# Gated linear attention and two mixture layers on one core: 32-wide column tiles in the attention step, and experts' places counted in steps of 8 tokens

## The chip, the cores and the metric

One core of a Trainium2 chip runs the whole program in one launch. The metric is the time of one execution in microseconds of device time. Of the kernel before, three timed runs are shown, and one profiled execution from which every row below is taken.

## The reference

Three layers follow one another over 3072 tokens (4 batches of 768) of 320 numbers (8 heads of 40).

1. A gated recurrence. For each head, a state `C` of 40 x 40 and a sum `n` of 40 are updated at every token, and the output is a ratio:

```
C = f_stab * C + i_stab * outer(v_t, k_t);   n = f_stab * n + i_stab * k_t
y_t = sigmoid(o_t) * (C @ q_t) / max(|n . q_t|, 1)
```

2. A dense layer: `h = x @ w_in` (320 to 1024), `h * softmax(h)`, a layer norm with the scale `g_ln`, `@ w_out` (1024 to 320).

3. A routed layer: each token goes to the one of 8 experts whose embedding has the largest cosine with it, and gets `gate * (relu(x @ w1[e]) @ w2[e])`, with the softmax of the scaled cosines as its gate.

Inputs and outputs are 32-bit floats.

## The kernel before, in words

**First half.** The sequence is cut into 24 chunks of 128 tokens (6 to a batch), and layers 1 and 2 are done chunk by chunk. For a chunk the recurrence becomes four groups of small fp32 matmuls on TensorE: `scores` (k against q, 128 x 128 for each head), `values` (the masked scores against the values, 41 columns with the row sum), `carried` (q against the state of the chunks before, 82 columns for two heads) and `outer` (k against the values, into the state). A matmul's output can stand on a part of the 128 partitions; that part is its column tile, and matmuls on different column tiles of the array can run beside each other. `values` and `carried` put a chunk's 128 tokens out in two halves of 64; `outer` puts the 40 rows of two heads at partitions 0 and 64. In the step `att` of the order, PE runs the rest of the dense layer's first product of an earlier chunk, then the next chunk's scores, then this chunk's values, carried state and outer product. The dense layer splits each operand in a high and a low part of the type fp32r and sums three products.

**Between the halves.** Tokens are routed in groups of 4 or 2 chunks (`r_best` to `r_add`). Each token's place within its expert is counted by matmuls with triangular matrices, and one-hot matmuls turn "token to place" into "place to token" (`inv`, from which `columns` reads gather indices). The experts are ranked by their count: the first two ranks by the count after 4 groups, the others by the final one (`rank_all`).

**Second half.** Each rank has a fixed number of places (`CAPS`, in units of `CW` = 32 tokens). A rank is a unit of work; rank 0 is two units, of which the first (384 tokens, `u0`) needs only the tokens of the first 5 groups, so it can start early. For a unit, rows of `ys` are gathered by an indirect DMA (`x_get`), transposed and split (`x_tr`, `x_hi`, `x_lo`); `m1` gives for each of 8 blocks `f` of the hidden layer 8 matmuls that stream the unit's tokens; `m1_hi` on ACT and `m1_lo` on DVE take the relu out of PSUM in two parts; `m2` gives for each tile of 128 tokens 24 matmuls that stream 320 columns; ACT applies the gate and an indirect DMA scatters the rows. Where a unit leaves a half tile of 64, the high and the low part of that half stand side by side as one 128-wide operand (16 matmuls instead of 24), and DVE adds the two halves of the result (`y_add`).

Tokens beyond the places are done by a loop at the end, that runs as often as a table on the chip says (`over_table`, 35 instructions on DVE, in the steps `otab`); with none left over, it runs no time.

**The order.** Every step is given to a plan with its engine and what it needs; the order in which they are issued is written out as numbers (`AT`, about 20 to a microsecond), and each engine runs its steps in that order. Steps that use the same PSUM bank wait for each other.

Of the kernel before, what the change touches and what calls it, by code (L numbers as in the profile page):

```python
# [9 lines left out]
F32 = mybir.dt.float32  # L10
F32R = mybir.dt.float32r
BF16 = mybir.dt.bfloat16
I32 = mybir.dt.int32
# [26 lines left out]
YW = XW + 1  # L40
# [5 lines left out]
CAPS = (16, 14, 14, 14, 12, 11, 11, 10)  # L46
CW = 32
NT = tuple(-(-x * CW // P) for x in CAPS)
# [3 lines left out]
NOVF = 32  # L52
GMAX = 40.0

C_ID, C_IOT, C_I192, C_I8, C_TOK, C_U, C_J, C_R, C_CAP, C_HCAP, C_TRI, C_GL, C_TAU = 0, 128, 256, 448, 456, 480, 608, 640, 648, 656, 664, 792, 800
NCONST = 801
# [4 lines left out]
EP = 32  # L61
FUSE = 2
# [1587 lines left out]
```

## Time and profile before

| | |
|---|---|
| median of 3 runs | 539.2 us (538.67 to 540.77) |
| profiled execution | 537.65 us |
| its span, first to last instruction | 535.7 us |
| busy share of PE, PEld (weight loads), DVE, ACT, POOL | 96%, 88%, 63%, 51%, 37% |
| TensorE clock granted | 0.994 of 2.4 GHz over the span |

PE is TensorE's matmul, PEld its weight loads, DVE VectorE, ACT ScalarE, POOL GpSimd, SP SyncE. A row of the timeline merges like instructions that follow one another: start, length from the first start to the last end, engine, line, output<-inputs, rows*columns of the weights and the shape streamed, and their count. Matmuls are pipelined: one lasts longer than the distance at which the next can start. L671 is line 671 of the kernel.

### The profile page before, as it was taken

What the parts mean: (1) busy time and instruction counts of PE and PEld (TensorE: products, weight loads), DVE (VectorE), ACT (ScalarE), POOL (GpSimd) and SP (SyncE); (2) the same over time, 40 slices, a digit from 0 to 9 for tenths busy, and PEclk for the clock granted to TensorE, in tenths of its full rate; (3) what the DMA queues carried; (4) which work ended last, traced back from release to release, by engine and by line L of the source; (5) the groups of instructions that cost most, each with busy time, mean ns of one, the idle gap of its engine ahead of it and who ended that gap; (6) DMA issues with size and microseconds to landing.
All of it is one profiled execution on the core that took longest, in us unless ns stands there. A gap on an engine that the chain in (4) does not pass through costs nothing. (4 is left out here: it accounts for less than half of the span.)

```text
span 535.7 us, 11869 instructions
## 1 busy us (share of the span) xinstructions
PE 512.6 (96%) x4600; PEld 470.5 (88%) x4600; DVE 339.5 (63%) x750; ACT 275.0 (51%) x601; POOL 198.0 (37%) x355
## 2 busy tenths in 40 slices
PE   5999999999999999999999889999999999999991
PEld 3778888999889999889998679899999999999991
DVE  6997756775667766667766867878463437554420
ACT  3464654655546574565547665454454345544420
POOL 2026222462174247226315864734243223202102
PEclk9999999999999999999999999999999999999997
DMA  8914423153242333314400631658364345723000
GB/s 335 406 44 139 130 78 117 50 167 111 81 133 80 118 116 128 125 38 136 169 1 1 217 114 61 201 176 253 106 187 157 104 124 176 249 54 129 13 20 31
DMA packets 20401, 67.95 MB, mean 127 GB/s; under 512 B 2635, under 2 KB 5779, under 8 KB 20336
## 3 DMA queue, kind: packets, MB, share of 16 engines
q1 hardware_dynamic: 17360, 58.14, 33.3%
q0 software_dynamic: 2976, 8.96, 5.1%
q8 instruction: 38, 0.62, 0.5%
q14 instruction: 27, 0.22, 0.1%
HBM read 58.43 MB, written 8.91 MB: 126 GB/s over the span
## 5 line engine op out<-in xcount | busy, mean ns | idle before, releaser
L1203 DVE SCALAR_TENSOR_TENSOR uu<-hpu,uu 128x384 fp32r<-128x384 f32 (+3 forms) x104 | 40.0, 415 | 55.2 <-ACT uu L1198 48.8
L1235 POOL DMA_INDIRECT out_x<-you,sidx x28 | 28.4, 1013 | 109.6 <-ACT you L1228 101.4
L1198 ACT ACTIVATE uu<-hpu 128x448 fp32r<-128x448 f32 (+4 forms) x72 | 33.9, 473 | 60.6 <-PE hpu L1186 53.0
L782 PE MATMUL Y<-OH,uh 128*128 128x328 f32 x192 | 63.4, 330 | 0.0
L1221 PE MATMUL ypu<-hr,uu 128*128 128x320 f32 (+1 forms) x192 | 59.8, 311 | 0.8 <-DVE uu L1203 0.8
L783 PE MATMUL Y<-OL,uh 128*128 128x328 f32 x192 | 60.0, 313 | 0.0
L784 PE MATMUL Y<-OH,ul 128*128 128x328 f32 x192 | 59.9, 312 | 0.0
L1223 PE MATMUL ypu<-hr,uu 128*128 128x320 f32 (+1 forms) x192 | 59.3, 309 | 0.0
L1222 PE MATMUL ypu<-lr,uu 128*128 128x320 f32 (+1 forms) x192 | 59.2, 309 | 0.0
L1140 DVE TENSOR_TENSOR lr<-wr,hr 128x1024 fp32r<-128x1024 f32 (+1 forms) x32 | 43.2, 1356 | 19.3 <-ACT hr L1133 18.4
L1182 PE MATMUL hpu<-exhr,hr 128*128 128x448 f32 (+4 forms) x144 | 49.6, 344 | 0.3 <-DVE uu L1203 0.3
L1184 PE MATMUL hpu<-exlr,hr 128*128 128x448 f32 (+4 forms) x144 | 48.0, 333 | 0.2 <-issue 0.2
L1183 PE MATMUL hpu<-exhr,lr 128*128 128x448 f32 (+4 forms) x144 | 48.0, 333 | 0.0
L1133 ACT CAST hr<-wr 128x1024 fp32r<-128x1024 f32 (+1 forms) x40 | 44.6, 1136 | 5.7 <-DMA wr<-in_w 1.6
L774 DVE TENSOR_TENSOR ul<-tpu,uh 128x512 fp32r<-128x512 f32 x48 | 32.5, 688 | 22.1 <-ACT uh L770 21.8
L733 DVE TENSOR_REDUCE nmx<-H 128x1 f32<-128x1024 f32 x24 | 29.3, 1222 | 25.7 <-PE H L729 23.7
L738 ACT ACTIVATE e<-H,nmx 128x1024 f32<-128x1024 f32 x24 | 26.8, 1116 | 36.6 <-DVE nmx L733 36.6
L720 PE MATMUL H<-WH,xh 128*128 128x512 f32 x96 | 39.9, 416 | 0.0
L1149 POOL DMA_INDIRECT xgr<-ys,gidx x28 | 31.6, 1129 | 18.5 <-DVE sidx L1070 6.6
L721 PE MATMUL H<-WL,xh 128*128 128x512 f32 x96 | 37.6, 391 | 0.0
L770 ACT CAST uh<-tpu 128x512 fp32r<-128x512 f32 x48 | 27.6, 587 | 18.4 <-PE tpu L766 17.3
L782 PEld LDWEIGHTS Y<-OH,uh 128*128 128x128 f32 x192 | 36.1, 188 | 0.8
(258 smaller groups left out, 1356.7 us busy)
## 6 DMA issues: line engine op xcount, KB each, us to landing
qk<-in_qkT SPq DMA_DIRECT2D x24, 512.0 KB
wr<-in_w SPq DMA_DIRECT2D x24, 512.0 KB
nat<-in_nat SPq DMA_DIRECT2D x24, 484.0 KB
wr<-in_w SPq DMA_DIRECT2D x16, 640.0 KB
ys<-yr SPq DMA_DIRECT2D x5, 770.0 KB
rawwo<-in_w_out SPq DMA_DIRECT2D x4, 640.0 KB
rawwi<-in_w_in SPq DMA_DIRECT2D x5, 512.0 KB
ys<-yr SPq DMA_DIRECT2D x2, 385.0 KB
```

The lines of the kernel that those rows point to most:

```text
L782: T.matmul(out=yp, lhsT=uh, rhs=OH[:, k, :], start=(k == 0), stop=False)
L783: T.matmul(out=yp, lhsT=uh, rhs=OL[:, k, :], start=False, stop=False)
L784: T.matmul(out=yp, lhsT=ul, rhs=OH[:, k, :], start=False, stop=(k == 7))
L1133: A.copy(out=R.h[i], in_=R.raw[i])
L1140: eng.tensor_tensor(out=R.l[i], in0=R.raw[i], in1=R.h[i].bitcast(F32), op=ALU.subtract)
L1182: T.matmul(out=o, lhsT=R.h[k][:, fs_], rhs=xh[:, k, tk], start=(k == 0), stop=False)
L1183: T.matmul(out=o, lhsT=R.l[k][:, fs_], rhs=xh[:, k, tk], start=False, stop=False)
L1184: T.matmul(out=o, lhsT=R.h[k][:, fs_], rhs=xl[:, k, tk], start=False, stop=False)
L1203: V.scalar_tensor_tensor(out=l_part(U, f, a, b), in0=U.us["p", f][:, a:b], scalar=0.0, in1=U.us["u", f][:, a:b].bitcast(F32), op0=ALU.max, ...
L1221: T.matmul(out=yp, lhsT=uh, rhs=hi, start=(f == 0), stop=False)
L1222: T.matmul(out=yp, lhsT=uh, rhs=lo, start=False, stop=False)
L1223: T.matmul(out=yp, lhsT=ul, rhs=hi, start=False, stop=(f == 7))
```

## The change

Four things, and with them a new set of numbers in `AT` (nearly every step of the second half and many of the first stand at other places).

1. `values`, `carried` and `outer` use column tiles of 32 instead of 64: four calls where there were two.
2. `CAPS` is in tokens, in multiples of 8. The remainder of a unit may be any width up to 64; its low part is put at column 64 of the operand. The unit `u1` (112 places) streams the high and the low part of x in one matmul, and adds the two results with one more step on ACT (`m1_part`) and one on DVE (`m1_sum`). In the last unit the split tile comes first.
3. `over_table` and its steps are gone; six small instructions say whether any expert has more tokens than places. If so, a loop runs every expert over every chunk with a mask (also used when the gates need the other path). For it, each row of `ys` has one more column, the expert's number.
4. Constants and tiles that only the table used are gone.

```diff
-CAPS = (16, 14, 14, 14, 12, 11, 11, 10)
-CW = 32
+CAPS = (496, 432, 448, 424, 360, 352, 328, 264)
+CT = [slice(EP * c, EP * c + EP) for c in range(4)]
...
     def values(s, num, stop):
         for p in range(NP):
             for r in range(2):
-                for j in range(2):
-                    T.matmul(out=num[halves(j), 2 * p + r, :], lhsT=s["Pt"][:, r, p, halves(j)], rhs=s["vp"][:, 2 * p + r, :], ...)
+                for q in CT:
+                    T.matmul(out=num[q, 2 * p + r, :], lhsT=s["Pt"][:, r, p, q], rhs=s["vp"][:, 2 * p + r, :], ...)
 
     def carried(s, num, c, start):
         for p in range(NP):
-            for j in range(2):
-                T.matmul(out=num[halves(j), 2 * p:2 * p + 2, :], lhsT=s["qk"][:QR, 0, p, halves(j)], rhs=c[:, p, :], ...)
+            for q in CT:
+                T.matmul(out=num[q, 2 * p:2 * p + 2, :], lhsT=s["qk"][:QR, 0, p, q], rhs=c[:, p, :], ...)
 
     def outer(s, stc, start, stop):
         for p in range(NP):
-            for r in range(2):
-                T.matmul(out=stc[HP * r:HP * r + D, p, :], lhsT=s["k"][:, 2 * p + r, :], rhs=s["vp"][:, 2 * p + r, :], ...)
+            for r, (a, b) in ((r, x) for r in range(2) for x in ((0, 32), (32, D))):
+                T.matmul(out=stc[HP * r + a:HP * r + b, p, :], lhsT=s["k"][:, 2 * p + r, a:b], rhs=s["vp"][:, 2 * p + r, :], ...)
...
-            self.half, self.lo = w % P == HP, EARLY * P if name == "u0" else 4 * P
+            self.left, self.lo, self.small = (w % P if w % P <= HP else 0), (EARLY if name == "u0" else 4) * P, w <= P
...
+        if U.small:
+            both = hp[:, :2 * U.w].rearrange("p (a t) -> p a t", a=2)
+            for k in range(2):
+                T.matmul(out=both, lhsT=R.h[k][:, fs_], rhs=R.x["b"][:, :, k, tk], start=(k == 0), stop=False)
+                T.matmul(out=o, lhsT=R.l[k][:, fs_], rhs=xh[:, k, tk], start=False, stop=False)
+            T.matmul(out=both, lhsT=R.h[2][:, fs_], rhs=R.x["b"][:, :, 2, tk], start=False, stop=True)
+            return
...
+    def m1_part(U, f):
+        U.us["s", f] = small.tile([P, P], F32, tag="hs", name=f"hs{U.name}_{f}", bufs=4)
+        A.copy(out=U.us["s", f][:, :U.w], in_=U.us["p", f][:, U.w:2 * U.w])
+
+    def m1_sum(U, f):
+        s_ = U.us["s", f][:, :U.w]
+        V.tensor_tensor(out=s_, in0=s_, in1=U.us["p", f][:, :U.w], op=ALU.add)
...
-            if both:
-                u = U.us["u", f][:, t0:t0 + P]
+            if both:
+                u = U.us["u", f][:, t0:t0 + HP + n]
                 T.matmul(out=yp, lhsT=u, rhs=hi, start=(f == 0), stop=False)
                 T.matmul(out=yp, lhsT=u, rhs=lo, start=False, stop=(f == 7))
...
+        jo = U.tiles if u < len(units) - 1 else (U.tiles[-1],) + U.tiles[:-1]
...
+    def too_many():
+        q, w = od["q"], ordw
+        V.tensor_tensor(out=q, in0=perm[:, 1].rearrange("p r c -> p c r"), in1=crow.unsqueeze(1).broadcast_to([P, E, E]), op=ALU.mult)
+        V.tensor_reduce(out=w[:, 0, :], in_=q, axis=AX.X, op=ALU.add)
+        V.tensor_tensor(out=w[:, 1, :], in0=w[:, 3, :], in1=w[:, 0, :], op=ALU.is_gt)
+        V.tensor_tensor(out=w[:, 1, :], in0=w[:, 1, :], in1=few, op=ALU.max)
+        V.tensor_reduce(out=w[:, 2, 0:1], in_=w[:, 1, :], axis=AX.X, op=ALU.max)
+        V.tensor_scalar(out=again, in0=w[0:1, 2, 0:1], scalar1=widef, scalar2=None, op0=ALU.max)
...
-            nv = nc.values_load(nov[0:1, 0:1], min_val=0, max_val=NOVF - 1)
-            with tc.For_i(0, nv, 1) as j:
...
+            with tc.For_i(0, E, 1) as e:
...
+                with tc.For_i(0, NG, 1) as g:
...
+                    V.scalar_tensor_tensor(out=part_of, in0=R.x[0][:, XE:YW], scalar=mine, in1=R.x[0][:, XW:XE], op0=ALU.is_equal, op1=ALU.mult)
...
+                    V.scalar_tensor_tensor(out=o, in0=U.us["y", 0][:, :DM], scalar=part_of, in1=o, op0=ALU.mult, op1=ALU.add)
```

## Rows read from the trace of the kernel before

**Rows 1.** The page's part 1: busy us (share of the span) xinstructions.

```profile
PE 512.6 (96%) x4600; PEld 470.5 (88%) x4600; DVE 339.5 (63%) x750; ACT 275.0 (51%) x601; POOL 198.0 (37%) x355
```

**Rows 2.** Windows: length, busy us (xcount) by engine, clock, DMA share, GB/s.

```profile
10.00:45.00 35.00, 34.93 (x376) 27.26 (x375) 32.77 (x55) 19.42 (x53) 9.86 (x9) 1.00 0.59 227
...
200.00:250.00 50.00, 50.00 (x531) 45.55 (x532) 33.50 (x81) 28.59 (x72) 22.51 (x48) 1.00 0.34 111
...
290.00:320.00 30.00, 25.96 (x163) 22.77 (x162) 23.39 (x54) 20.66 (x43) 21.20 (x35) 1.00 0.45 147
...
450.00:500.00 50.00, 50.00 (x333) 49.67 (x332) 28.29 (x38) 26.67 (x43) 7.30 (x8) 1.00 0.44 137
```

**Rows 3.** PE's waits: who waited <- releaser: us, times, longest.

```profile
PE ip L875 <- POOL ohv L869: 1.6, 1, 1.6
PE txr L1160 <- DMA xgr<-ys,gidx: 1.5, 1, 1.5
```

**Rows 4.** Timeline of PE in one chunk's attention step: start us, us, what.

```profile
207.77 1.13 PE L671 MATMUL num<-nat,Pt 128*64 128x41 f32 x32
208.72 0.77 PE L676 MATMUL num<-Cb,qk 104*64 104x82 f32 x16
209.32 0.48 PE L681 MATMUL stc<-nat 128*40 128x41 f32 x16
209.73 0.42 PE L782 MATMUL Y<-OH,uh 128*128 128x328 f32 x1
```

**Rows 5.** Groups by form: rows*columns of weights, streamed, xcount | busy us, mean ns.

```profile
L671 PE MATMUL num<-nat,Pt 128*64 128x41 f32 x768 | 27.2, 231 | 0.0
L676 PE MATMUL num<-Cb,qk 104*64 104x82 f32 x320 | 15.4, 238 | 0.0
L681 PE MATMUL stc<-nat 128*40 128x41 f32 x320 | 9.6, 202 | 0.0
...
L553 PE MATMUL wep<-wt,enT 128*32 128x128 f32 x32 | 1.3, 279 | 0.0
...
L671 PEld LDWEIGHTS num<-nat,Pt 128*64 128x64 f32 x768 | 24.3, 138 | 3.8 <-ACT OH L600 0.8 <-issue 0.4
...
L553 PEld LDWEIGHTS wep<-wt,enT 128*32 128x32 f32 x32 | 0.8, 109 | 0.2
```

**Rows 6.** wep, on four column tiles: timeline, then a window of 0.03 us.

```profile
16.14 1.00 PE L553 MATMUL wep<-wt,enT 128*32 128x128 f32 x24
...
16.14:16.17 0.03, 0.03 (x4) 0.03 (x4) 0.00 (x0) 1.00 0.78 307
```

**Rows 7.** Timeline of m1: a block's matmul and the next block's, 8 matmuls on.

```profile
347.40 0.28 PE L1183 MATMUL hpu<-exhr,lr 128*128 128x128 f32 x1
...
348.29 0.28 PE L1183 MATMUL hpu<-exhr,lr 128*128 128x128 f32 x1
...
425.31 0.36 PE L1182 MATMUL hpu<-exhr,hr 128*128 128x448 f32 x1
...
426.93 0.37 PE L1182 MATMUL hpu<-exhr,hr 128*128 128x448 f32 x1
...
500.55 0.31 PE L1182 MATMUL hpu<-exhr,hr 128*128 128x320 f32 x1
...
501.72 0.31 PE L1182 MATMUL hpu<-exhr,hr 128*128 128x320 f32 x1
```

**Rows 8.** Groups by form of the small unit's passes out of PSUM.

```profile
L1198 ACT ACTIVATE uu<-hpu 128x128 fp32r<-128x128 f32 x8 | 2.1, 278 | 6.2 <-PE hpu L1186 2.7 <-issue 1.8 <-PE txr L1160 1.7
...
L1203 DVE SCALAR_TENSOR_TENSOR uu<-hpu,uu 128x128 fp32r<-128x128 f32 x8 | 2.1, 288 | 3.5 <-ACT uu L1198 3.3
```

**Rows 9.** Timeline of DVE: first and last of 12 instructions of the table.

```profile
341.74 0.15 DVE L1308 TENSOR_SCALAR ovi<-cp 128x8 int32<-128x8 f32 x1
...
343.85 0.29 DVE L1322 SCALAR_TENSOR_TENSOR ovt<-few,ovt 128x8 f32<-128x8 f32 x2
```

**Rows 10.** Timeline of the end: the add of the last split tile.

```profile
525.49 0.55 DVE L1232 SCALAR_TENSOR_TENSOR you<-ypu,xgater,you 64x320 f32<-64x320 f32 x1 [7.29 <-issue]
```

More of the change, by code (lines that the diff above doesn't have):

```diff
@@ L271, in moe_kernel @@
     sidx = const.tile([P, E, 4], U32, name="sidx")
-    ga_all = const.tile([P, NV], U32, name="ga_all")
-    sa_all = const.tile([P, NV], U32, name="sa_all")
-    tabi = const.tile([P, 2, NOVF], I32, name="tabi")
-    nov = const.tile([P, 1], I32, name="nov")
-    wide = const.tile([1, 2], I32, name="wide")
+    wide = const.tile([1, 1], I32, name="wide")
     widef = const.tile([1, 1], F32, name="widef")
@@ L857, in r_key @@
         k = small.tile([P, 3, n], I32, tag="key", name="key" + name)
[L858 removed]
+        V.scalar_tensor_tensor(out=k[:, 0, :], in0=s["yr"][:, :, XE], scalar=float(N), in1=t[:, :, 5], op0=ALU.mult, op1=ALU.add)
         V.tensor_single_scalar(out=k[:, 1, :], in_=k[:, 0, :], scalar=7, op=ALU.arith_shift_right)
@@ L1010, in moe_kernel @@
         add(("rgate", c), "V", lambda s=s: r_gate(s), after=[("rexp", c)] + [("ry", g) for g in gs])
-        add(("st_y", c), "S", lambda c=c, s=s: SY.dma_start(out=ys[G0[c] * P:G0[c + 1] * P].rearrange("(b p) w -> p b w", p=P), in_=s["yr"]), after=[("rgate", c)], size=197 * n)
+        add(("st_y", c), "S", lambda c=c, s=s: SY.dma_start(out=ys[G0[c] * P:G0[c + 1] * P].rearrange("(b p) w -> p b w", p=P), in_=s["yr"]), after=[("rgate", c), ("ridx", c)], size=197 * n)
         add(("pos", c), "P", lambda s=s, q=q: r_place(s, q, "T"), after=[("ridx", c), "mk"] + ([("count", c - 1)] if c else []), take="T")
@@ L1142, in part @@
     def part(r, j):
-        return min(P, CAPS[r] * CW - j * P)
+        return min(P, CAPS[r] - j * P)
     def x_get(R, j, ix, rows=N, n=P):
@@ L1153, in x_gate @@
         n = R.x["n", j]
-        G.tensor_copy(out=R.x["g", j][:n], in_=R.x[j][:n, XW:YW])
+        G.tensor_copy(out=R.x["g", j][:n], in_=R.x[j][:n, XW:XE])
     def x_tr(R, j):
@@ L1168, in x_lo @@
     def x_lo(R, j):
-        if "l" not in R.x:
-            R.x["l"] = pools[R.pool].tile([P, 3, 4 * P], F32R, tag="exl", name=f"exl{R.name}")
         n = R.x["n", j]
@@ L1186, in m1, with hidden_of @@
         T.matmul(out=o, lhsT=R.h[2][:, fs_], rhs=xl[:, 2, tk], start=False, stop=True)
-    def l_part(U, f, a, b):
-        u = U.us["u", f]
-        if U.half and a == U.w - HP:
-            return u[:, U.w:U.w + HP]
-        return u[:, U.lo + a:U.lo + b]
+    def m1_part(U, f):
[4 more added lines that the diff above has]
+        V.tensor_tensor(out=s_, in0=s_, in1=U.us["p", f][:, :U.w], op=ALU.add)
+    def hidden_of(U, f):
+        return U.us["s", f] if U.small else U.us["p", f]
     def m1_hi(U, f):
@@ L1197, in m1_hi @@
         U.us["u", f] = pool.tile([P, w], F32R, tag=f"u{f}", name=f"u{U.name}_{f}")
-        A.activation(out=U.us["u", f][:, :U.w], in_=U.us["p", f][:, :U.w], func=AF.Relu)
+        A.activation(out=U.us["u", f][:, :U.w], in_=hidden_of(U, f)[:, :U.w], func=AF.Relu)
     def m1_lo(U, f):
-        w = U.w
-        for a, b in ((0, w - HP), (w - HP, w)) if U.half else ((0, w),):
-            V.scalar_tensor_tensor(out=l_part(U, f, a, b), in0=U.us["p", f][:, a:b], scalar=0.0, in1=U.us["u", f][:, a:b].bitcast(F32), op0=ALU.max, op1=ALU.subtract)
+        u, p, w = U.us["u", f], hidden_of(U, f), U.w
+        for a, b, o in ((0, w - U.left, U.lo), (w - HP, w, HP)) if U.left else ((0, w, U.lo),):
+            V.scalar_tensor_tensor(out=u[:, o + a:o + b], in0=p[:, a:b], scalar=0.0, in1=u[:, a:b].bitcast(F32), op0=ALU.max, op1=ALU.subtract)
     def m2(R, U, j, h, tag):
@@ L1209, in m2 @@
         t0 = (j - U.tiles[0]) * P
-        both = U.half and n == HP
-        yp = U.us["y", j][:2 * n if both else n, :DM]
+        both = n == U.left
+        yp = U.us["y", j][:HP + n if both else n, :DM]
         for f in range(4 * h, 4 * h + 4):
@@ L1231, in y_add @@
         n, yo = R.x["n", j], U.us["o", j]
-        V.scalar_tensor_tensor(out=yo[:n], in0=U.us["y", j][n:2 * n, :DM], scalar=R.x["g", j][:n], in1=yo[:n], op0=ALU.mult, op1=ALU.add)
+        V.scalar_tensor_tensor(out=yo[:n], in0=U.us["y", j][HP:HP + n, :DM], scalar=R.x["g", j][:n], in1=yo[:n], op0=ALU.mult, op1=ALU.add)
     def y_put(U, j, ix, n=P):
@@ L1236, in y_put @@
         i = getattr(i, "ins", i)
-        if U.name != "o":
-            if pools.get("sc"):
-                tc.declare_no_dep(i, group="rows", reason="every token has a row of its own")
-            tc.add_to_no_dep_group("rows", i)
-            pools["sc"] = True
+        if pools.get("sc"):
+            tc.declare_no_dep(i, group="rows", reason="every token has a row of its own")
+        tc.add_to_no_dep_group("rows", i)
+        pools["sc"] = True
     ranks = [Rank(r, f"r{r}") for r in range(E)]
-    units = [Unit(0, tuple(range(EARLY)), EARLY * P, "u0"), Unit(0, tuple(range(EARLY, NT[0])), CAPS[0] * CW - EARLY * P, "u1")]
-    units += [Unit(r, tuple(range(NT[r])), CAPS[r] * CW, f"u{r + 1}") for r in range(1, E)]
+    units = [Unit(0, tuple(range(EARLY)), EARLY * P, "u0"), Unit(0, tuple(range(EARLY, NT[0])), CAPS[0] - EARLY * P, "u1")]
+    units += [Unit(r, tuple(range(NT[r])), CAPS[r], f"u{r + 1}") for r in range(1, E)]
+    assert units[1].small
     ytag = 0
@@ L1279, in moe_kernel @@
             add(("m1", u, f), "P", lambda R=R, U=U, f=f, htag=htag: m1(R, U, f, htag), after=[("xb", r, j) for j in U.tiles] + [("wo", r, i) for i in range(3)] + lo_us + ["open_f"] * (htag is None), war=([("m1", u, f - 1)] if f else [("m1", u - 1, 7)] if u else []), take=htag or "F")
-            add(("ma", u, f), "A", lambda U=U, f=f: m1_hi(U, f), after=[("m1", u, f)] + lo_us, war=wu)
-            add(("mb", u, f), "V", lambda U=U, f=f: m1_lo(U, f), after=[("ma", u, f)] + lo_us, war=wu, give=[(("m1", u, f), 0)])
-        for j in U.tiles:
+            summed = ("ms", u, f) if U.small else ("m1", u, f)
+            if U.small:
+                add(("mx", u, f), "A", lambda U=U, f=f: m1_part(U, f), after=[("m1", u, f)], war=[("mb", u, f - 4)] if f > 3 else [])
+                add(summed, "V", lambda U=U, f=f: m1_sum(U, f), after=[("mx", u, f)], give=[(("m1", u, f), 0)])
+            add(("ma", u, f), "A", lambda U=U, f=f: m1_hi(U, f), after=[summed] + lo_us, war=wu)
+            add(("mb", u, f), "V", lambda U=U, f=f: m1_lo(U, f), after=[("ma", u, f)] + lo_us, war=wu, give=[] if U.small else [(("m1", u, f), 0)])
+        jo = U.tiles if u < len(units) - 1 else (U.tiles[-1],) + U.tiles[:-1]
+        for ji, j in enumerate(jo):
             tag = (("st", "num") if u == 0 else ("Y", "st", "num"))[ytag % (2 if u == 0 else 3)]
@@ L1285, in moe_kernel @@
             for h in range(2):
-                add(("m2", u, j, h), "P", lambda R=R, U=U, j=j, h=h, tag=tag: m2(R, U, j, h, tag), after=[("mb", u, f) for f in range(4 * h + 4)] + [("wo", r, 3 + x) for x in range(h + 1)] + ([("m2", u, j, 0)] if h else []), war=([("m2", u, j - 1, h)] if j > U.tiles[0] else [("m2", u - 1, units[u - 1].tiles[-1], h)] if u else []) + ([("m1", 0, 7)] if u == 0 else []), take=() if h else tag)
+                add(("m2", u, j, h), "P", lambda R=R, U=U, j=j, h=h, tag=tag: m2(R, U, j, h, tag), after=[("mb", u, f) for f in range(4 * h + 4)] + [("wo", r, 3 + x) for x in range(h + 1)] + ([("m2", u, j, 0)] if h else []), war=([("m2", u, jo[ji - 1], h)] if ji else [("m2", u - 1, units[u - 1].tiles[-1], h)] if u else []) + ([("m1", 0, 7)] if u == 0 else []), take=() if h else tag)
             yorder.append((u, j))
-            both = U.half and part(r, j) == HP
+            both = part(r, j) == U.left
             nb = BUFS["yo"]
@@ L1355, in table_space @@
-    def table_space(pool):
-        return [pools[pool].tile([P, NOVF, E], F32, tag=t, name=n) for t, n in (("ovle", "le"), ("ovlo", "lo"))]
-    def ocnt():
-        od["ocnt"] = bank("T", "cp", (P, E))
-        T.matmul(out=od["ocnt"], lhsT=onebf, rhs=cum, start=True, stop=True)
-    add("ocnt", "P", ocnt, after=[("count", NGR - 1), ("invm", NGR - 1)], take="T")
-    def otab(i):
-        if i == 0:
-            od["otab"] = over_table(od["ocnt"], table_space("L"), True)
-        next(od["otab"], None)
@@ L1368, in moe_kernel @@
-    for i in range(6):
-        add(("otab", i), "V", lambda i=i: otab(i), after=[("otab", i - 1)] if i else ["ocnt", "open_l", "rank2", "badc"], give=[] if i else [("ocnt", 0)])
-    add("zero", "G", lambda: (G.memset(cum, 0.0), G.memset(inv, 0.0)), after=[("otab", 5), "col_4"])
+    def too_many():
[6 more added lines that the diff above has]
+        V.tensor_scalar(out=again, in0=w[0:1, 2, 0:1], scalar1=widef, scalar2=None, op0=ALU.max)
@@ L1372, in moe_kernel @@
+    add("over", "V", too_many, after=["rank2", "few", "badc"])
     for k in plan.order():
@@ L1533, in redo @@
                 SY.dma_start(out=ys.rearrange("(b c p) w -> b p c w", c=NCH, p=P)[bass.ds(bi, 1)].rearrange("b p c w -> (b p) c w"), in_=t["yr"])
-                r_place(t, "g", "T")
-                r_own(t)
-                r_count(t)
-                r_key(t, "g")
-                for c in range(NCH):
-                    r_hot(t, c, V, tk[:, c:c + 1], "g")
-                    r_invert(t, c, c == 0, c == NCH - 1, "g", "st")
-                r_add(t)
-            n1 = nc.values_load(wide[0:1, 0:1], min_val=0, max_val=1)
-            with tc.For_i(0, n1, 1):
-                cnt = bank("T", "gcnt", (P, E))
-                T.matmul(out=cnt, lhsT=onebf, rhs=cum, start=True, stop=True)
-                for _ in over_table(cnt, table_space("sg"), False):
-                    pass
     left = nc.values_load(again[0:1, 0:1], min_val=0, max_val=1)
@@ L1569, in moe_kernel @@
+            G.memset(acc, 0.0)
+            with tc.For_i(0, E, 1) as e:
+                R = Rank(0, "o")
+                mine = small.tile([P, 1], F32, name="mine", bufs=1)
+                V.tensor_copy(out=mine, in_=cs[:, bass.ds(e + C_I8, 1)])
                 for i in range(5):
-                    w_load(R, ev, i)
+                    w_load(R, e, i)
                     w_hi(R, i)
                     w_lo(R, i, V)
-                for f in range(8):
-                    m1(R, U, f)
-                    m1_hi(U, f)
-                    m1_lo(U, f)
@@ L1577, in moe_kernel @@
-                for h in range(2):
-                    m2(R, U, 0, h, "Y")
-                y_out(R, U, 0)
-                y_put(U, 0, ix[:, 1:2])
+                with tc.For_i(0, NG, 1) as g:
+                    U = Unit(0, (0,), P, "o")
+                    R.x = {("n", 0): P}
+                    R.x[0] = pools["R"].tile([P, YW], F32, name="oxg")
+                    SY.dma_start(out=R.x[0], in_=ys.rearrange("(t p) w -> t p w", p=P)[bass.ds(g, 1)].rearrange("a p w -> (a p) w"))
+                    part_of = small.tile([P, 1], F32, name="partof", bufs=1)
+                    V.scalar_tensor_tensor(out=part_of, in0=R.x[0][:, XE:YW], scalar=mine, in1=R.x[0][:, XW:XE], op0=ALU.is_equal, op1=ALU.mult)
+                    x_tr(R, 0)
+                    x_hi(R, 0)
+                    x_lo(R, 0)
+                    U.small = False
+                    for f in range(8):
+                        m1(R, U, f)
+                        m1_hi(U, f)
+                        m1_lo(U, f)
+                    for h in range(2):
+                        m2(R, U, 0, h, "Y")
+                    o = acc[:, bass.ds(g * DM, DM)]
+                    V.scalar_tensor_tensor(out=o, in0=U.us["y", 0][:, :DM], scalar=part_of, in1=o, op0=ALU.mult, op1=ALU.add)
```

113 lines of the change are left out of this document (20 added, 93 removed), and 258 rows, old and new, of the table AT.

## The prediction

> **What bounds the kernel now.** Read the page's busy table first [rows 1]: PE 96% of the span. Then the windows [rows 2]: where the chunks run (200 to 250 us) PE is busy in all 50 us at a granted clock of 1.00, DVE in 33.5 and ACT in 28.6, so PE sets the pace. From 10 to 45 us DVE, which decodes weights, is busy in 32.8 of 35 us; what PE saves there is worth nothing. From 290 to 320 us PE stands idle for 4 of 30 us. The list of PE's waits [rows 3] names two of them: a one-hot on POOL, and the first gather of tokens. So a shorter PE stream is a shorter kernel, except before 45 us and between the last chunks and the first full expert.
>
> A busy PE is not PE at its peak, so the next view is the timeline of one chunk's attention step [rows 4], with the mean length of one instruction from the groups by form [rows 5]. A row's length less one instruction is the time from the first start to the last. The 32 pairs of weight load and matmul in the values step (L671; 16 calls, each fp32 call shows as two pairs) take 1.13 - 0.23 = 0.90 us for 31 intervals, 29.0 ns each. Two column tiles run side by side, so one step of two takes 58 ns. Carried state (L676): (0.77 - 0.24)/15 = 35.3 ns, a step of 71. Outer product (L681): (0.48 - 0.20)/15 = 18.7 ns, a step of 37. Values and outer product stream the same 41 columns; they differ in the weights, 64 columns against 40. So the values step is set by its weight load, the carried state (82 columns, 64-column weights, 71 ns) by its stream.
>
> **The change, part by part.** Sums go against the profiled execution, 537.65 us (span 535.7); the median of the runs shown is 539.2, 1.55 above, and the forecast is put on that median.
>
> *Values on four tiles of 32.* 16 calls become 32: 64 pairs, but 16 steps of four as there were 16 of two. Weights are 32 columns; the loads shorten with the columns, 138 ns at 64 and 109 at 32 [rows 5]. The nearest row for such a step is the outer product's: same stream, 40-column weights, 37 ns. Lower bound: weights alone scaled to 32 columns, 30 ns. Upper bound: the only four-tile row here, wep. Its 24 pairs start (1.00 - 0.28)/23 = 31 ns apart, 125 ns a step for 128 columns, with one change from 128 to 64 rows inside [rows 6]; were 22 ns of that the price of four tiles instead of two, a step would be 59 and the gain nothing. I take 37: the first four pairs of wep begin within 30 ns of each other, so four do start together, below 37. Gain 16 x (58 - 37) = 0.34 us a chunk. Chunks 0 and 1 lie before 45 us; 22 x 0.34 = 7.4 us (bounds 0 and 9.9).
>
> The Trainium skill speaks against this step: TensorEngine Tiling (Array Packing), section Instruction Overhead, says that every matmul carries about 60 cycles, one of a single column lasting as long as one of 60, and that no tiling should be taken from a dimension that is small already. By it a step of 41 columns is paid as 60, about 50 ns at the rate of two cycles a column that the carried step shows, and the gain would be 2.8 us instead of 7.4; the outer product's 37 ns is under that, so I go by the row.
>
> *Carried state and outer product* double their calls (32 pairs each) and keep 8 steps at 71 and 37 ns, both about stream time: 0. They have to use 32 columns too, or the array would change its shape inside the burst. The price if four starts don't fit in 37 ns is the third rival.
>
> *Places by 8 tokens.* First-layer matmuls (m1) stream a unit's width. 448 columns: 1.62 us for 8, 202 ns; 320: 1.17 us, 146 ns [rows 7]; the slope is 0.44 ns a column. New widths: 432 for 448, 424 for 448, 360 for 384, 328 for 352, 264 for 320: 16 + 24 + 24 + 24 + 56 = 144 columns, times 64 matmuls a unit: 4.0 us. 264 would be 122 ns, still above the 111 ns where the weights bind. The second layer (m2) streams 320 whatever the places, and keeps 640 matmuls, since the same four units have a remainder up to 64 (48, 64, 40 and 8 tokens). DVE and ACT are far from busy there (28 and 27 of 50 us at 450 to 500 us): nothing else takes over. Bounds 3 to 4.5.
>
> *The small unit (128, now 112 places).* Eight matmuls per f at 0.89 us, 111 ns each [rows 7], become five: high and low half of x run in one stream of 224 columns (0.44 ns a column: 105 ns), so the weights bind and each stays 111 ns. 64 - 40 = 24 matmuls, 2.7 us. Added per f: a copy on ACT and an add on DVE of the kind in [rows 8] (0.28, 0.29 us), between the matmul and the release of one of two PSUM buffers. A buffer is then held for 0.28 (matmul) + 0.28 + 0.29 us and two hand-offs, about 1.1; half of it is 0.55, as long as five matmuls. Near a tie: +0.5 us (bounds 0 and 3).
>
> *The overflow table goes.* 35 small DVE instructions, 12 of them in a row from 341.74 to 344.1 us [rows 9], ahead of a split that the next unit's matmuls wait for; six take their place. They lie beside PE work; what shows is part of PE's last waits: -0.5 (0 to -1). The new loop does not run: counted from the reference's inputs, the experts hold 495, 426, 441, 420, 360, 346, 322 and 262 tokens in the order of the places (496, 432, 448, 424, 360, 352, 328, 264).
>
> *The end.* The last unit's split tile moves ahead, so the add on DVE (0.55 us, [rows 10]) leaves the path from the last matmul to the last scatter: -0.6, against 128 rows in the last scatter instead of 64 (0 to -0.9).
>
> *Given back.* Between the last chunks and the first full expert PE waits for chains on POOL, DVE and DMA that get no shorter [rows 3]. PE's filler there shrinks by about five chunks x 0.34 = 1.7 and the small unit's 2.7. No row shows slack, so all 4.4 us return (bounds 0 and 6; the moved places of nearly every step may mend or add a wait there, and I find no sign in the rows).
>
> Wider rows of ys (386 for 385), a constant block 40 columns shorter, a store that waits for an index already made: nothing, hidden behind the 96% of PE; without cover some 0.1 us each.
>
> Sum: -7.4 - 4.0 - 2.7 + 0.5 - 0.5 - 0.6 + 4.4 = -10.3: 527.35 in a profiled execution, **528.9** on the median.
>
> **Rivals.**
> *All of it lands.* Nothing is given back and a values step takes 30 ns: -9.9 - 4.0 - 2.7 - 0.5 - 0.6 = -17.7, 521.5. For it: 100% PE in the chunks. Against: the waits of [rows 3] stand where PE would run ahead. 0.16.
>
> *Four tiles are no faster than two.* If the four loads share one path, a values step stays at 58 ns: 7.4 less gain, 1.7 less given back, -4.6: 534.6. For it: no row shows four narrow loads bound by themselves (wep hides them under 128 columns). Against: two 64-column loads side by side do not stretch each other (138 ns, on a straight line with 109 at 32). 0.14.
>
> *The start of a pair is the bound (slower).* In the burst of a chunk, 64 pairs become 128. If PE can begin a pair only every x ns, the burst takes 128x against 16 x 58 + 8 x 71 + 8 x 37 = 1.79 us. The closest sustained starts in the trace are the outer product's 18.7 ns; if that is a floor and not its stream, values cost 1.20 instead of 0.93, carried 0.60 for 0.57, outer 0.60 for 0.30: +0.60 us x 22 = 13.2, with the rest (-7.3, and 2.7 of it given back) +8.6: 547.8. It turns the kernel slower from about x = 1.79/128 + 4.6/(22 x 128) = 15.6 ns. Against: four starts in 30 ns in wep, though only in short bursts. 0.09.
> The Trainium skill's TensorE: Matmul & The Clock Gate, section "Wait — 56ns, not 53.3ns?", gives this as a rule, starts never under about 25 ns; by it the burst would take 3.2 us and the time would be some 565. The 18.7 ns of the outer product's starts are below it, so for different column tiles the trace does not agree.
>
> *The seam eats it.* The chain from the last chunk's routing to the gathers sets the second half's start and the new order adds a wait: 5 more given back, -5.3 or less, up to -2: 534 to 537. 0.08.
>
> *It doesn't do what it says.* One expert sits at its 360 places exactly; one more token there runs the masked loop: 8 experts x 24 groups x (64 x 0.111 + 24 x 0.147 us) is over 2,000 us. 0.02.
>
> **How the numbers follow.** The forecast has 0.51. Its own range, with the bounds above, is 524 to 533. The whole range is 522.5 to 535: it leaves out half of the first rival, the third and the last. Under 0.5% (2.7 us) a measurement cannot tell from no change. Faster: 0.51 + 0.16 + 0.13 + 0.04 = 0.84; same 0.05; slower 0.11.
>
> **What would show it.** Values row: 64 pairs in about 0.59 + 0.23 us; 0.9 means the second rival, 1.2 the third. Carried and outer rows at 0.77 and 0.48 us. The last chunk's values begin about 7 us earlier. From the first matmul of the 448-wide unit (432 after) to the last matmul of all, about 4 us less. PE's waits between the last chunks and that matmul about 4 us more. A kernel whose chunks keep their length, or whose second half starts no earlier than before, proves me wrong.

## The result, and the profile after

The changed kernel takes **526.07 us** (median of 4 runs, 525.21 to 527.22) against 538.93 (median of 4, 537.83 to 540.77) beside it: ratio **0.976**, 95% interval 0.972 to 0.980. Beside the later experiments it was timed once more: 525.34 against 537.0, ratio 0.9785 (0.9767 to 0.9803). The forecast was 528.9, with a range of 522.5 to 535. The profiled execution took 525.21 us, its span is 523.5 us, and the mean granted clock is 0.994, as before.

The page's busy table (engine, busy us, share of the span, instructions) is to be read against [rows 1]:

```profile
PE 500.5 (96%) x5983; PEld 456.8 (87%) x5983; DVE 333.3 (64%) x727; ACT 275.5 (53%) x609; POOL 201.1 (38%) x353
```

PE has 1,383 more instructions and is busy for 12.1 us less; the span shrank by 12.2. Its idle time is about what it was: all of the gain is shorter PE work. The windows (length, then busy us of PE, PEld, DVE, ACT and POOL, clock, DMA share, GB/s) answer to [rows 2]:

```profile
200.00:250.00 50.00, 49.74 (x769) 44.86 (x769) 32.62 (x79) 28.42 (x70) 24.41 (x45) 1.00 0.36 115
290.00:320.00 30.00, 27.58 (x171) 24.04 (x171) 22.27 (x62) 18.55 (x41) 23.59 (x41) 1.00 0.44 129
450.00:500.00 50.00, 50.00 (x345) 49.62 (x344) 23.72 (x39) 22.76 (x43) 8.47 (x8) 1.00 0.31 97
```

PE still sets the pace in the chunks and in the second half. Between them it idled 4.0 of 30 us before and 2.4 after. PE's waits between 280 and 360 us (who <- releaser: us, times, longest) answer to [rows 3]:

```profile
PE hpu L1178 <- DVE uu L1204: 1.6, 2, 0.9
PE ip L865 <- POOL ohv L859: 1.0, 1, 1.0
PE txr L1150 <- DMA xgr<-ys,gidx: 0.5, 1, 0.5
```

The one-hot on POOL and the gather are waited for less (1.6 and 1.5 before). The longest wait is now that of the first product's matmuls (`hpu`, L1178) for the step on DVE that empties the PSUM tile they need (L1204, it writes `uu`): 1.6 us, where 0.3 stood before, beside 0.8 of the second product. The waits changed place, and PE's idle time in this stretch fell from 5.3 to 4.1 us.

One chunk's attention step on PE (start, length, what), to be read against [rows 4]:

```profile
203.44 0.82 PE L661 MATMUL num<-nat,Pt 128*32 128x41 f32 x64
204.07 0.77 PE L666 MATMUL num<-Cb,qk 104*32 104x82 f32 x32
204.64 0.49 PE L671 MATMUL stc<-nat 128*32 128x41 f32 x32
205.06 0.66 PE L756 MATMUL tpu<-cs,u 128*128 128x128 f32 x4
```

The values row fell from 1.13 to 0.82 us with twice the pairs, and the other two kept their length (0.59 + 0.23, 0.77 and 0.48 had been forecast). From the first values matmul to the next step's first it is 1.62 us (203.44 to 205.06) against 1.96 before (207.77 to 209.73). The groups by form (weights, streamed, xcount | busy us, mean ns of one) answer to [rows 5]; the last three are the small unit's:

```profile
L661 PE MATMUL num<-nat,Pt 128*32 128x41 f32 x1536 | 19.7, 202 | 0.0
...
L661 PEld LDWEIGHTS num<-nat,Pt 128*32 128x32 f32 x1536 | 16.7, 110 | 3.1 <-issue 0.4
...
L1173 PE MATMUL hpu<-exr,hr 128*128 128x224 f32 x16 | 4.3, 323 | 0.2
L1174 PE MATMUL hpu<-exr,lr 128*128 128x112 f32 x16 | 3.6, 224 | 0.0
L1175 PE MATMUL hpu<-exr,hr 128*128 128x224 f32 x8 | 2.6, 325 | 0.0
```

To see where the time went, four places are read from the timeline: the first values matmul of the last chunk, the first matmul of the first full expert (448 wide before, 432 after), the last matmul of all, and the last scatter. First before, then after:

```profile
287.13 1.13 PE L671 MATMUL num<-nat,Pt 128*64 128x41 f32 x32
...
356.59 0.45 PE L1182 MATMUL hpu<-exhr,hr 128*128 128x448 f32 x1
...
524.45 0.31 PE L1218 MATMUL ypu<-lr,uu 128*128 128x320 f32 x1
...
526.32 0.91 POOL L1235 DMA_INDIRECT out_x<-you,sidx  x1 [0.79 <-DVEq L1550]
```

```profile
281.64 0.82 PE L661 MATMUL num<-nat,Pt 128*32 128x41 f32 x64
...
347.66 0.36 PE L1178 MATMUL hpu<-exr,hr 128*128 128x432 f32 x1
...
512.25 0.31 PE L1224 MATMUL ypu<-hr,uu 128*128 128x320 f32 x1
512.64 0.53 ACT L1229 ACTIVATE you<-ypu,xgater 128x320 f32<-128x320 f32 x1 [2.99 <-PEq L1476]
513.45 0.98 POOL L1236 DMA_INDIRECT out_x<-you,sidx  x1 [2.38 <-ACTq L1476]
```

The same places in the other profiles give the lengths of four stretches, in us. "Chunks" runs from the values of the third chunk to those of the last, the "seam" from there to the first full expert, the "second half" from there to the last matmul. The last column is PE's idle time from 280 to 360 us.

| kernel | before the chunks | chunks | seam | second half | end | span | idle |
|---|---|---|---|---|---|---|---|
| before | 49.53 | 237.60 | 69.46 | 167.86 | 11.29 | 535.7 | 5.3 |
| after | 50.37 | 231.27 | 66.02 | 164.59 | 11.20 | 523.5 | 4.1 |
| before + the three on 32 | 50.63 | 231.37 | 69.35 | 167.85 | 11.63 | 530.8 | 5.6 |
| after, old order | 49.50 | 231.49 | 66.81 | 163.62 | 11.29 | 522.7 | 6.0 |
| the same, eight matmuls | 49.42 | 231.50 | 67.84 | 163.60 | 11.17 | 523.5 | 4.9 |
| after, old places | 50.92 | 232.01 | 66.68 | 168.58 | 11.17 | 529.4 | 4.6 |

### The profile page after: what moved, and what is told of

It reads as the page before. It is cut to its first block, busy times and chain, and to the rows that moved or that the text cites. A ratio compares the mean times of both kernels' runs of the same rounds, so it can differ in the third digit from the quotient of the medians.

```text
span 523.5 us, 14615 instructions
## 1 busy us (share of the span) xinstructions
PE 500.5 (96%) x5983; PEld 456.8 (87%) x5983; DVE 333.3 (64%) x727; ACT 275.5 (53%) x609; POOL 201.1 (38%) x353
## 5 line engine op out<-in xcount | busy, mean ns | idle before, releaser
L1204 DVE SCALAR_TENSOR_TENSOR uu<-hpu,uu 128x384 fp32r<-128x384 f32 (+4 forms) x96 | 37.3, 420 | 50.4 <-ACT uu L1198 46.0
L1198 ACT ACTIVATE uu<-hpu 128x384 fp32r<-128x384 f32 (+7 forms) x64 | 30.8, 483 | 57.4 <-PE hpu L1182 51.7
L1222 PE MATMUL ypu<-hr,uu 128*128 128x320 f32 (+4 forms) x192 | 59.5, 310 | 0.0
L1223 PE MATMUL ypu<-lr,uu 128*128 128x320 f32 (+4 forms) x192 | 59.3, 309 | 0.0
L1224 PE MATMUL ypu<-hr,uu 128*128 128x320 f32 (+4 forms) x192 | 59.3, 309 | 0.0
L1130 DVE TENSOR_TENSOR lr<-wr,hr 128x1280 fp32r<-128x1280 f32 (+1 forms) x32 | 43.2, 1357 | 17.1 <-ACT hr L1123 16.4
L1178 PE MATMUL hpu<-exr,hr 128*128 128x384 f32 (+7 forms) x128 | 44.0, 344 | 1.6 <-DVE uu L1204 1.6
L1180 PE MATMUL hpu<-exr,hr 128*128 128x384 f32 (+7 forms) x128 | 42.5, 332 | 0.0
L1179 PE MATMUL hpu<-exr,lr 128*128 128x384 f32 (+7 forms) x128 | 42.5, 332 | 0.0
L773 PEld LDWEIGHTS Y<-OL,uh 128*128 128x128 f32 x192 | 36.2, 188 | 0.5 <-issue 0.5
```

Of the source, the lines that this page charges most:

```text
L773: T.matmul(out=yp, lhsT=uh, rhs=OL[:, k, :], start=False, stop=False)
L1130: eng.tensor_tensor(out=R.l[i], in0=R.raw[i], in1=R.h[i].bitcast(F32), op=ALU.subtract)
L1178: T.matmul(out=o, lhsT=R.h[k][:, fs_], rhs=xh[:, k, tk], start=(k == 0), stop=False)
L1179: T.matmul(out=o, lhsT=R.l[k][:, fs_], rhs=xh[:, k, tk], start=False, stop=False)
L1180: T.matmul(out=o, lhsT=R.h[k][:, fs_], rhs=xl[:, k, tk], start=False, stop=False)
L1222: T.matmul(out=yp, lhsT=uh, rhs=hi, start=(f == 0), stop=False)
```

## The experiments

Ratios are to the kernel before, with 95% intervals. The theory after this result: each part shortened PE's own work, and the seam gave nothing back. Rivals: the forecast's return at the seam is there and was paid for by something else; or the new order closed the seam.

**Column tiles alone.**

```diff
-for j in range(2): T.matmul(out=num[halves(j), ...], lhsT=s["Pt"][:, r, p, halves(j)], ...)
+for q in CT:       T.matmul(out=num[q, ...], lhsT=s["Pt"][:, r, p, q], ...)   # carried, outer likewise
```

> The kernel before with one thing changed: values, carried state and outer product on column tiles of 32; order, widths, table and tail as before. Theory: a values step costs 39.4 ns instead of 58 (64 pairs from 203.44 in 0.82 us after, 32 in 1.13 us before), on the path in 22 chunks, 16 x 18.6 ns = 0.30 us a chunk, 6.5 us, and the seam between the last chunks and the first full expert gives nothing back: 6 to 7 us under the kernel before. Rival A (the forecast's own step): the seam's waits are fixed in time, the filler lost there comes back as a wait, -5 us or less, and PE's stalls between the last chunks and the 448-wide expert grow by 1.7 us. Rival B: the order that was rewritten with the change is what keeps the seam short, so that this kernel in the old order gains 4 us or less.

531.73 us, ratio 0.9879 (0.9862 to 0.9896): 6.5 us less. Its timeline at the two ends of the seam:

```profile
282.00 0.82 PE L672 MATMUL num<-nat,Pt 128*32 128x41 f32 x64
...
351.35 0.45 PE L1183 MATMUL hpu<-exhr,hr 128*128 128x448 f32 x1
```

The last chunk comes 5.1 us earlier and the first full expert 5.2: the seam keeps its 69.4 us, and idle time there grew by 0.25 us, not by the 1.7 that rival A and the forecast had. PE's two long waits in it, before and here, show why (in brackets: the idle time ahead of the row, and what ended it):

```profile
301.78 0.36 PE L875 MATMUL ip<-ohv,ohr 128*128 128x192 f32 x1 [1.61 <-POOL ohv L869]
...
313.38 0.85 PE L1160 MATMUL txr<-cs,xgr 128*128 128x128 f32 x6 [1.48 <-DMA xgr<-ys,gidx]
```

```profile
296.34 0.36 PE L876 MATMUL ip<-ohv,ohr 128*128 128x192 f32 x1 [1.63 <-POOL ohv L870]
...
308.16 0.85 PE L1161 MATMUL txr<-cs,xgr 128*128 128x128 f32 x6 [1.70 <-DMA xgr<-ys,gidx]
```

Both end 5.2 to 5.4 us earlier, as the last one-hot on POOL (300.72 and 295.28) and the gather (304.33 and 298.89) start 5.4 us earlier: the chains moved with the chunks. Over the 22 chunks the sum from first values matmul to next step is 40.16 us before and 32.69 here, 7.5 less. The chunks' stretch holds 21 of these bursts, 7.1 us less, and became 6.2 us shorter: some 0.9 us came back, most of it as idle time of PE in that stretch (1.0 us of 231.4, 0.3 of 237.6 before). The profiled execution is the slowest of the four, and its span is only 4.9 us shorter because its stretch before the chunks is 1.1 us longer; that stretch takes from 49.0 to 51.3 us in the profiles of this case. This is the largest part of the gain, and it needs none of the new order.

**Values alone on 32.** The same edit in `values` only.

> The kernel before with values alone on column tiles of 32, carried state and outer product on 64 as they were. The prediction said that these two have to follow or the array changes its shape inside the burst. If that change has a price, two of them are added per chunk (values to carried, and the outer product no longer follows tiles of 32); other shape changes in the trace of after cost 130 to 200 ns (last outer matmul to the next full-width one), so 0.13 to 0.2 us of the 0.30 us a chunk are lost and the gain over the kernel before is 2 to 4 us. If a change from 32 to 64 columns costs no more than any next step, the gain is that of the kernel with all three on 32, 6 to 7 us.

534.17 us, ratio 0.9938 (0.9925 to 0.995): 3.3 us less, half of the full edit's gain. One chunk:

```profile
205.79 0.82 PE L672 MATMUL num<-nat,Pt 128*32 128x41 f32 x64
206.54 0.79 PE L677 MATMUL num<-Cb,qk 104*64 104x82 f32 x16
207.16 0.47 PE L682 MATMUL stc<-nat 128*40 128x41 f32 x16
```

The values row is as short as after, yet the carried state starts 0.75 us behind its first matmul instead of 0.63 (203.44 to 204.07). From the last values matmul to the first of the carried state it is 0.13 us here, 0.05 before with both on tiles of 64, and 0.01 after with both on 32: the change from 32 to 64 shows there. The carried state itself then takes 0.62 us (206.54 to 207.16) where it takes 0.57 after. From the first values matmul to the next step it is 1.78 us, and 1.62 after. So the two edits that were put at nothing earn about 0.16 us a chunk: they keep the shape.

**The kernel after with all three back on 64.**

> The kernel after with values, carried state and outer product back on column tiles of 64, all else as after. Theory: 22 x 0.30 = 6.5 us over the kernel after, 532 to 533. Rival: the seam absorbs part of it (the forecast's 1.7 us), so that only about 5 us come back. If the tiles are worth nothing and the new order carries the gain, it stays within 1 us of the kernel after.

534.64 us, ratio 0.9934 (0.9917 to 0.995), 8 to 9.4 us over after by its two ratios, where 6.5 were expected. The chunks are 6.3 us longer (237.55), as before the change. The rest lies ahead of the chunks (51.31) and behind them (PE idles 5.6 us between 280 and 360): in this order one edit taken out moves waits elsewhere too. Undoing a part says less here than adding it to the old kernel.

**The old places.**

```diff
-CAPS = (496, 432, 448, 424, 360, 352, 328, 264)
+CAPS = (512, 448, 448, 448, 384, 352, 352, 320)
```

> The kernel after with the places as before (512, 448, 448, 448, 384, 352, 352, 320). Theory: 144 more columns streamed by 64 matmuls a unit, at the 0.44 ns a column of the prediction 4.0 us over the kernel after; the two traces side by side gave 3.3 us from the first matmul of the 448-wide unit to the last unit's second layer. The small unit is 256 columns instead of 224 in its merged matmuls: 16 matmuls with weights bound or stream bound, up to 0.2 us more. Expected 3.3 to 4.2 us over after. Rival: DVE, ACT or the weights bind in part, 2 us or less.

530.41 us, ratio 0.9857 (0.9841 to 0.9872). The second half grows from 164.59 to 168.58 us, 4.0, the forecast's number. The whole is 3.9 to 5.3 us over after, depending on which of after's two ratios is taken; what is beyond 4.0 lies ahead of the second half (chunks and seam 0.7 us each), where one profile cannot tell it from chance: after's own second profile has chunks of 232.35 us.

**Eight matmuls for the small unit, in the new order.**

```diff
-..., self.small = ..., w <= P
+..., self.small = ..., False
```

> The kernel after with the small unit's first layer as before: eight matmuls per f, no copy on ACT and no add on DVE to join the two halves. Theory: 24 matmuls more at 111 ns each, 2.7 us, less the 0.5 us that the added hops were given: 2.2 us over after, if the seam shows it. Rival: in the trace of after the small unit's merged matmuls stand in blocks with waits of 0.42 to 0.47 us for ACT and DVE, so the merged form is bound by its evacuation and undoing it costs 1 us or less, or gains. Second rival: the filler is worth nothing there because the waits behind it are fixed in time: 0 +- 0.5 us.

534.06 us, ratio 0.994 (0.992 to 0.996), some 8 to 10 us over after. None of the three theories has that. The mean clock is 0.981 to 0.987 in all six runs, and windows around the small unit show where it fell (PE busy, PEld, DVE, ACT, POOL, clock):

```profile
340.00:343.00 3.00, 2.34 (x22) 2.21 (x20) 1.19 (x4) 1.30 (x4) 2.39 (x3) 1.00 0.92 324
343.00:346.00 3.00, 3.00 (x22) 2.81 (x22) 1.59 (x5) 1.08 (x4) 2.46 (x6) 0.72 0.84 324
346.00:349.00 3.00, 2.80 (x14) 2.62 (x13) 0.20 (x1) 0.16 (x1) 2.42 (x4) 0.50 0.39 107
...
352.00:355.00 3.00, 3.00 (x16) 3.00 (x15) 0.36 (x2) 0.26 (x1) 0.00 (x0) 0.57 0.00 0
```

PE had idled 1.3 us between 335 and 343 us, 0.63 for a gather and 0.66 for the DVE step that writes `uu`; then TensorE ran at its 1.2 GHz level (0.50) until about 354 us. In the windows shown from 343 us on PE is busy nearly throughout, at half of its clock in one of them. The seam is 73.96 us long, 7.9 more than after, of which 24 matmuls at 111 ns explain 2.7. The run tells what a fall of the clock costs in this order, and not what the merging is worth.

**The old order.** The new kernel with the places in the order of the kernel before.

> The kernel after with each step's place in the order written out by hand as in the kernel before (the few new steps put in at the nearest places). Theory: the seam's stalls are short because the new order fits the shorter filler; with the old one the forecast's 4.4 us are given back, 4 to 5 us over after. Rival: the seam's chains move with the chunks and need no new order: within 1 us of after.

524.47 us, ratio 0.976 (0.9746 to 0.9773): the rival. The rewritten order is worth nothing that can be measured: the seam is 0.8 us shorter in it, and the second half 1.0 longer.

**The old order, eight matmuls.** The undoing again, where the clock holds.

> The kernel after in the order of the kernel before, with the small unit's first layer as eight matmuls per f again, no copy and no add. The same undoing in the new order cost about 10 us, with the granted clock at 0.50 to 0.72 from 343 to 355 us. Theory: that was the clock and not the matmuls; in the old order the clock stays at 1.00 (as in the kernel with the tiles alone, which has the same unmerged unit), the stretch from the last chunk's values to the first 432-wide matmul grows from 66.8 to about 69.4 us, and the time is 2.5 to 3 us over the same order with the merged unit (524.5): 527. Rival: the waits behind the small unit are fixed, 524.5 to 525. Second rival: fewer matmuls there are worth 10 us whatever the order, 534.

526.16 us, ratio 0.9801 (0.9788 to 0.9814), 2.2 us (give or take 1.0) over the same order with five matmuls, near what was expected; the two profiles differ by 0.8 us of span, and the seam by 1.0 (66.81 to 67.84 us), where 2.6 had been expected. The clock is 1.00 throughout the seam. PE idles 4.9 us there, with five matmuls 6.0: of 24 matmuls fewer, part came back as waiting. PE's waits with five matmuls, in the old order:

```profile
PE txr L1150 <- DMA xgr<-ys,gidx: 1.7, 1, 1.7
...
PE txr L1150 <- PE hpu L1175: 0.7, 1, 0.7
```

With eight, the second of these is gone and the first is 1.3 us.

**Less filler.**

```diff
-T.matmul(out=o, lhsT=R.l[k][:, fs_], rhs=xh[:, k, tk], ...)   # in the small unit's five
```

> The kernel after with the two low-order matmuls per f of the small unit's first layer left out (16 matmuls of 112 columns, about 1.8 us of PE's stream; the low half of the weights is missing in that unit's first layer). It asks whether what PE does between the last chunks and the first full expert is filler for chains that end at a fixed time. If the small unit lies behind those chains' ends (theory, from the seam that gave nothing back), the time falls by up to 1.8 us. If its block is bound by the ACT copy and the DVE add (waits of 0.42 to 0.47 us in it), nothing changes. If less work there lets the clock fall, it is slower by several us.

524.92 us, ratio 0.9779 (0.9766 to 0.9793), beside after's 0.9785 on the same chip: 0.4 us of 1.8, and even that is within the intervals. PE's waits between 280 and 360 us show where the rest is:

```profile
PE txr L1150 <- DMA xgr<-ys,gidx: 1.4, 2, 0.9
...
PE hpu L1173 <- DVE hsu L1189: 0.8, 2, 0.4
```

The gather is waited for 0.9 us longer than in after, and PE's matmuls wait 0.8 us for the merged unit's add on DVE, which is not among after's waits of PE in that stretch. Both had been named: here most of what the filler lost is given back, and a block of three matmuls waits for its evacuation.

The kernel after, timed beside this run, was to lie at 0.974 to 0.978 of the kernel before if the single edits (6.5 us, 4 and 2.5) add up; 0.9785 (0.9767 to 0.9803) is at the edge of that, and far from the 0.972 or less that the undoings of 8 to 10 us would have meant.

**The table late, in the kernel before.** `ocnt`, `otab` and `zero` at 8050 to 8700 in the order instead of 6625 to 7452.

> The kernel before with the 35 small vector instructions of its overflow table, and the two count steps around it, placed some 18 us later, behind the seam. Theory as predicted: the table's 2.4 us on DVE ahead of a split show as 0.5 us of PE's last waits: 0.5 us under the kernel before. Rival: the table is what held the split, so that all of the seam's relief (up to 3 us) comes from its going: 2 to 3 us under. Second rival: 0, because PE's waits there end on POOL and DMA.

537.11 us, ratio 0.9996 (0.9983 to 1.0009): no gain that can be measured. The interval leaves room for 0.9 us, so the forecast's 0.5 stays open; the rival's 2 to 3 us are out, as far as moving the table tells of taking it away. The profile is of the slowest of the 12 executions (539.41). Two windows of it:

```profile
312.00:316.00 4.00, 1.70 (x11) 1.46 (x11) 2.27 (x7) 2.53 (x7) 2.26 (x7) 0.91 0.20 74
316.00:320.00 4.00, 4.00 (x21) 3.96 (x20) 1.46 (x5) 1.18 (x5) 1.92 (x6) 0.66 0.01 4
```

PE stood still for 2.3 of 4 us, waiting for a gather, and the clock fell there and in the next four. Whether it did so in the other executions no profile shows; their mean clocks are 0.992 or more, beside 0.990 in this one. From the kernel with the tiles alone to the one in the old order with eight matmuls the seam shrinks by 1.5 us; table, places and smaller copies share that, and no run separates them.

**What sets a four-tile step.** The filler matmuls of the preparing stage became bursts of 16 steps.

> The kernel after, with its 48 filler matmuls in the preparing stage (results unused) replaced by bursts of 16 steps: four tiles of 32 columns streaming 8, 41 or 82 columns, two tiles of 64 streaming 8 or 41, and four tiles with 8-column weights streaming 8. Its time is not the point, the start-to-start time of a step in each burst is. If the stream sets a step at 0.84 to 0.9 ns a column (carried state: 71 ns for 82 columns), four tiles with 41 columns take 37 to 39 ns, with 82 70 to 72, and with 8 columns the weights of 32 bind at about 30 ns (half of the 58 ns of two 64-column tiles). If the four starts bind, four tiles take the same 39 ns at 8 and at 41 columns, and with 8-column weights too. Two tiles of 64 take 58 ns at 8 and at 41 columns if the weights set it; less at 8 if the stream did.

This one missed: its edit gave all bursts the form of two 64-column tiles with 41 columns, 29.15 ns a pair. The second run has the six forms:

> The burst measurement again, with the six forms that the earlier run was to have (there all bursts took the form of two 64-column tiles streaming 41 columns: 58.3 ns a step, the two starts 6 to 7 ns apart and the next step 51 to 52 ns later). If the stream sets a step, four tiles of 32 take 37 to 40 ns with 41 columns, 70 to 72 with 82 and about 30 with 8 columns (weights); if the four starts set it, 8 and 41 columns take the same 39 ns, and 8-column weights change nothing. Two tiles of 64 streaming 8 columns: 58 ns if their weights set the step, 30 to 40 if not.

Its timeline, where the granted clock was 1.00 (windows 53 to 60, 60 to 69 and 69 to 72 us); rows end where PE paused:

```profile
54.29 1.26 PE L627 MATMUL H<-cs 128*32 128x8 f32 x128
...
57.86 1.42 PE L630 MATMUL H<-cs 128*32 128x41 f32 x128
59.08 2.01 PE L633 MATMUL H<-cs 128*32 128x82 f32 x101
...
65.67 2.04 PE L636 MATMUL H<-cs 128*64 128x8 f32 x64
67.56 2.05 PE L639 MATMUL H<-cs 128*64 128x41 f32 x64
69.53 0.76 PE L642 MATMUL H<-cs 128*8 128x8 f32 x75
```

Read as in the prediction (length less one instruction, over the intervals), a step of four takes 34 ns with 8 columns, 38 with 41 and 71 with 82; a step of two with 64-column weights takes 58 at 8 and at 41 columns. So the old values step was set by its weights. The new one lies just above two bounds: its share of the 82-column stream, 71 x 41/82 = 35.5 ns, and what four starts need. With 8-column weights and 8 columns a step begins at 25 ns and settles at 33 (medians over its starts), 8.2 ns a pair, the same as with 32-column weights. The stream is the nearer of the two.

## Why the prediction was right

**Values (7.4 forecast).** The reading "set by the weights, not the stream" holds: 58 ns with 64-column weights whatever the stream, and 38 to 39 ns for the new step (0.82 - 0.20 = 0.62 us for 63 intervals), where the outer product's 37 was taken. Over 22 chunks the bursts became 40.16 - 32.72 = 7.44 us shorter. That it meets the 7.4 is in part luck: 16 steps of 58 - 39.4 ns are 0.30 us a chunk, 6.5 us, and the rest was won where the carried state joins (0.05 us after the last values matmul before, 0.01 after). The chunks' stretch, with 21 of the bursts (7.1 us), became 6.3 shorter: 0.8 us came back as idle time of PE there (1.2 us, 0.3 before), which the sum had no term for.

**Carried state and outer product (0).** Right, and so was the reason for them: left on 64 they cost some 0.16 us a chunk, half of the gain.

**Places (4.0).** 3.3 in the new order, 4.2 in the old one (167.86 to 163.62), 4.0 when only the places are undone.

**The small unit (2.7, less 0.5).** In the old order it is worth 0.8 us by the profiles and 2.2 by the timed runs. The hop over ACT and DVE shows where a near tie was forecast; of the stops of weight loads in the small unit's blocks this one names it:

```profile
341.55 0.19 PEld L1173 LDWEIGHTS hpu<-exr,hr 128*128 128x128 f32 x1 [0.28 <-DVE hsu L1190]
```

**The table (0.5)** was not measured by itself; between nothing and 1.5 us fits the runs.

**The end (0.6)** is the step that was right and worth nothing: the last scatter ends 2.19 us after the last matmul starts instead of 2.78, but the program's end follows it by 9.02 us instead of 8.51. The whole end is 11.20 us against 11.29. The bound of 0 was in the text.

**Given back (4.4): the term that was mis-sized.** The prediction put it so: "No row shows slack, so all 4.4 us return". For the tiles, 0.25 of 1.7 us came back there. The waits of that stretch start from the results of the chunks that were counted as filler: with the chunks earlier, the chain through POOL and the gather is 5.4 us earlier too, and the seam keeps its length (69.46 and 69.35 us). For the small unit, whose matmuls do stand beside the next gather, 1.1 us came back beside the 1.0 that was kept (old order), and in the run with less filler most of 1.8. PE's idle time there fell from 5.3 to 4.1 us (it rose to 6.0 in the old order) instead of growing by 4. The last chunk's values begin 5.5 us earlier, where 7 had been named.

So of the 4.4 us some 1.4 are seen to come back in the seam. The 0.8 that came back in the chunks, and the end's 0.6 that did not show, make up for a part of the difference. Errors of either sign are in the sum, and that the total gain, 11.5 to 12.9 us by the two ratios, comes within 1.2 to 2.6 us of the forecast's 10.3 is better than its last term deserves. Of the seam's 3.4 us, some 1.5 were won by table, places and smaller copies together, with no run that parts them.

**The rivals.** "All of it lands" (521.5) took the right side on the tiles, though with a step of 30 ns that was not met, and the wrong one on the small unit. "The seam eats it" fell: the seam became 3.4 us shorter. "No faster than two" and the slower one, starts as the bound, are settled by the bursts: four tiles take 38 ns against 58, and a pair can start every 8.2 ns, where 15.6 would have decided against the change. The Trainium skill's TensorE: Matmul & The Clock Gate, section "Wait — 56ns, not 53.3ns?", has 25 ns as the least distance of two starts; for pairs on different column tiles no run here agrees. The Trainium skill's TensorEngine Tiling (Array Packing), section Instruction Overhead, would have a 41-column step cost as much as one of 60; the bursts do not agree: the step of 38 ns beside 34 with 8 columns and 71 with 82 shows a floor near 33 ns for four tiles, which the 41 columns clear.

## What to carry to other kernels

Compare two groups that stream the same columns with different weights: if the wider weights are slower, narrower column tiles can be worth their doubled instructions, as long as the step stays above what its starts need (33 ns for four here). Narrow all groups of a burst together, since a change of tile width between them took half of what one of them had won. Before a gain is booked as "given back" at a wait, ask from which event the waited-for chain starts: if it is released by the work that became shorter, it moves along, and only work that stands beside the chain after its start is lost. The places fit the counts of these inputs with 0 to 7 tokens to spare; no run shows the kernel on others.

## What the runs showed that was not expected

With 8-column weights, four column tiles took a pair of weight load and matmul every 6.3 ns in the first eight steps of a burst, and every 8.2 ns from there on. The clock is the risk in such a seam. In six profiles of kernels with PE idle for 5.3 to 6.0 us between 280 and 360 us (before, tiles alone, values alone, after with all three on 64, after in the old order, less filler) it stayed at 1.00 there. In two others (eight matmuls in the new order, 6.3 us; the table late, 5.7 us) it fell to 0.50 or 0.66 for some microseconds, at a price of several in the first. In both, the fall came right behind waits of PE, 1.3 us within 8 and 2.3 us within 4. But neither the total of idle time nor such a cluster tells which kernel it strikes: the kernel with the tiles alone idled 2.6 us between 292 and 300 us, at 1.00 all the time. What sets the fall stays open.
